# Last stage of a three-part kernel: PSUM split as four single banks and two pairs instead of two and three, and the last tile's output in two halves

## The chip, the cores and the metric

The kernel runs on one core of one Trainium2 chip. The metric is device time in microseconds (us) of one execution, the median of several runs. TensorE (PE) multiplies matrices into PSUM, which has eight banks of 512 fp32 values per partition here; VectorE (DVE) and ScalarE (ACT) read PSUM and work on tiles in SBUF; SyncE's queue (SP) issues the DMAs.

## The reference

Three parts follow each other: a block-causal attention (4 batches, 8 heads, 576 positions), a mixture of four experts over its 2304 output rows, and a feed-forward block with a SoLU and a layer norm, which is the last stage here:

```python
def _moe2_ref(x, w_in, w_out, g_ln) -> np.ndarray:
    h = x @ w_in                                  # 2304x512 @ 512x1024
    h_max = np.max(h, axis=-1, keepdims=True)
    e = np.exp(h - h_max)
    sm = e / (np.sum(e, axis=-1, keepdims=True) + 1e-09)
    solu = h * sm
    mu = np.mean(solu, axis=-1, keepdims=True)
    var = np.mean((solu - mu) ** 2, axis=-1, keepdims=True)
    ln = (solu - mu) / np.sqrt(var + 1e-06) * g_ln
    return (ln @ w_out).astype(np.float32)        # 2304x1024 @ 1024x512
```

## The kernel before

The 2304 rows are 18 tiles of 128. All products are made of fp16 pairs (a high and a low part), three matmuls for each product. The expert stage before the last one ends with second products of expert 3 (`emit_o`, L394, tiles named `ops`), which VectorE adds to the tile's sum (`out_unit`, L419, `acc`). ScalarE and VectorE then split that sum into an fp16 pair (L470, L471, `xh`), and a DMA transposes it to `x2T`, the input of the last stage. The PSUM tiles of the expert stage lie in a pool of three banks (`psh`, banks 0 to 2) and one of five (`psb`, banks 3 to 7); both are closed before the last stage opens its own two pools over the same banks, in the order in which they are written: `pso` first, then `ps2`.

The last stage runs over the 18 tiles t. `m2_h(t)` makes h: 24 matmuls of 512 columns (L1432) into a pair of banks of `ps2`. VectorE takes the maximum (L1438, `mx`) and a bias (L1442, `nb`); ScalarE the exponential with its sum (L1445, `ex`); VectorE the product h times ex (L1447, `raw`), which is the last reader of the pair. Then VectorE does the statistics (L1450, L1452), a chain of small instructions for the inverse root (L1455 to L1477), the normalisation (L1478), and with ScalarE the fp16 split (L1483 high part, L1484 low part, `lh`). SyncE issues the transposing DMA to `lt`. The tiles `ex`, `raw` and `lh` have two buffers each (pool `mp`), so `raw` of tile t+2 goes where `raw` of tile t lay until L1484 has read it. `m2_o(t)` makes the output: 24 matmuls (L1495) into a bank of `pso`, ScalarE copies it out with a scale (L1498, `o2s`), and SyncE issues the DMA to `out`. `m2_o` runs four tiles behind `m2_h` in the program (`OLAG = 4`).

A scheduler puts the instructions of each engine into a fixed order when the kernel is built; on the chip each engine takes its own instructions in that order and waits where an operand or a buffer isn't ready. I call the h of tile t h0, h1, ..., the output o0, o1, ..., and in the same way mx0, ex0, raw0, lh0, lt0. Before, `pso` holds banks 0 and 1, and the three pairs of `ps2` are banks 2-3, 4-5 and 6-7.

Of the kernel before, what the change touches and what calls it, by code (L numbers as in the profile page):

```python
# [7 lines left out]
F32 = mybir.dt.float32  # L8
# [6 lines left out]
AF = mybir.ActivationFunctionType  # L15
ALU = mybir.AluOpType
AX = mybir.AxisListType
PSUM = bass.MemoryType.PSUM

NB, NH, S, HD = 4, 8, 576, 64  # L20
NT, D, F, E = 2304, 512, 1024, 4
KD, KF = D // 128, F // 128
NTILE = NT // 128
# [14 lines left out]
TILES = [(0, 0), (2, 0)] + [(b, i) for b in range(NB) for i in range(1, 5)]  # L38
# [22 lines left out]
def tile_kernel(  # L61
# [16 lines left out]
    pe = nc.tensor  # L78
# [21 lines left out]
    vec, act, gp, sync = nc.vector, nc.scalar, nc.gpsimd, InOrder(nc.sync)  # L100
# [1129 lines left out]
    def norm():  # L1230
# [11 lines left out]
        w=p0[:5], x=p1[:5], W=p0[5:] + q0, X=p1[5:] + q1, P=[norm],  # L1242
        S=[lambda: at1.v_square(z0, 0, keep=True), lambda: at1.v_scale(z0, 1), lambda: at1.v_split(z0, 0)],
# [101 lines left out]
    while at1.more:  # L1345
        t, u, cost = moe[-1] if moe else (-1, None, 0)
        ok = t is None or t in ready and len(bg) <= n1
        if not ok or tdv <= tpe + 2.0:
            flush()
            at1.step()  # L1350
            a, c = at1.cost()
# [63 lines left out]
    mp = ctx.enter_context(tc.tile_pool(name="m2", bufs=2))  # L1415
    tp_ = ctx.enter_context(tc.tile_pool(name="lt", bufs=4))
    phs.close()
    pso = ctx.enter_context(tc.tile_pool(name="pso", bufs=2, space=PSUM))
    ps2 = ctx.enter_context(tc.tile_pool(name="ps2", bufs=3, space=PSUM))
    osc = sq.tile([128, 1], F32, tag="osc", name="osc")  # L1420
    vec.tensor_scalar_mul(osc, iw[:, 2 * len(LOADS) + 1:2 * len(LOADS) + 2], 1.0 / LSC)
    lnT = {}
# [64 lines left out]
        lnT[t] = tt  # L1487

    def m2_o(t):
        ps = pso.tile([128, 512], F32, tag="o2", name="o2")  # L1490
        tt, w = lnT.pop(t), wt["w_out"]
        m = 0
        for f in range(KF):
            for a, b in ((0, 0), (0, 1), (1, 0)):
                pe.matmul(ps, tt[:, a * KF + f], w[:, b, f], start=(m == 0), stop=(m == 3 * KF - 1))  # L1495
                m += 1
        o = ep.tile([128, 512], F32, tag="ev", name="o2s")
        act.activation(out=o, in_=ps, func=AF.Copy, scale=osc)  # L1498
        b, i = TILES[t]
        if i == 0:  # L1500
            for j in range(2):
                sync.dma_start(out=out[(b + j) * S:(b + j) * S + 64], in_=o[64 * j:64 * j + 64])
        else:
            r0 = b * S + 64 + 128 * (i - 1)
            sync.dma_start(out=out[r0:r0 + 128], in_=o)

    for t in range(NTILE + OLAG):
        if t < NTILE:
            m2_h(t)
        if t >= OLAG:  # L1510
            m2_o(t - OLAG)
# [69 lines left out]
```

## Time and profile before

| what | us |
|---|---|
| median of 3 runs (1112.07 to 1114.56) | 1113.18 |
| the profiled execution | 1114.37 |
| its span, first to last instruction | 1112.6 |
| PE busy | 1048.0 (94%) |
| DVE busy | 797.7 (72%) |
| ACT busy | 514.1 (46%) |
| POOL busy | 182.1 (16%) |

The profiled execution lasts 1.8 us longer than its span, and 1.2 us longer than the median of the runs. Times of instructions below are counted from the start of the span. "Busy" of PE is modelled from overlapping matmuls: one of 512 columns is shown with 379 ns, while 24 of them in a row take 5.18 us, 216 ns each. The granted clock is the share of TensorE's full speed (2.4 GHz) that it was given.

### The profile page before, as it was taken

What the parts mean: (1) busy time and instruction counts of PE and PEld (TensorE: products, weight loads), DVE (VectorE), ACT (ScalarE), POOL (GpSimd) and SP (SyncE); (2) the same over time, 40 slices, a digit from 0 to 9 for tenths busy, and PEclk for the clock granted to TensorE, in tenths of its full rate; (3) what the DMA queues carried; (4) which work ended last, traced back from release to release, by engine and by line L of the source; (5) the groups of instructions that cost most, each with busy time, mean ns of one, the idle gap of its engine ahead of it and who ended that gap; (6) DMA issues with size and microseconds to landing.
All of it is one profiled execution on the core that took longest, in us unless ns stands there. A gap on an engine that the chain in (4) does not pass through costs nothing.

```text
span 1112.6 us, 20532 instructions
## 1 busy us (share of the span) xinstructions
PE 1048.0 (94%) x8064; PEld 657.2 (59%) x8064; DVE 797.7 (72%) x1758; ACT 514.1 (46%) x1107; POOL 182.1 (16%) x176
## 2 busy tenths in 40 slices
PE   4579889799999999999999999999999999999998
PEld 4456666465555556555576767666667674444443
DVE  7898788738768677436677656674879558999883
ACT  5667676646755455433443424232446453333222
POOL 4874633422115421000000000000000000000000
PEclk9999989799999999999999999999999999999999
DMA  9868987928877857332531212330344311434333
GB/s 303 247 164 159 249 184 163 222 79 192 193 120 178 177 147 157 64 61 48 174 114 58 77 39 76 115 133 29 95 138 128 107 27 29 95 86 88 74 85 85
DMA packets 225600, 137.95 MB, mean 124 GB/s; under 512 B 184544, under 2 KB 192736, under 8 KB 225504
## 3 DMA queue, kind: packets, MB, share of 16 engines
q1 hardware_dynamic: 225504, 136.65, 50.2%
q8 instruction: 63, 1.03, 0.4%
q14 instruction: 33, 0.27, 0.1%
HBM read 79.47 MB, written 12.06 MB: 82 GB/s over the span
## 4 chain that ended last, share of the span: by engine, by line
PE 75%; DMA 9%; DVE 7%; POOL 4%; issue 2%; ACT 2%; SPq 0%; ACTq 0%; DVEq 0%; POOLq 0%
PE ops L394 29%; PE hps L626 13%; PE hps L372 11%; PE h L1432 8%; PE o L1495 8%; DMA pT<-hl 6%; PE pv L993 3%; PE sps L912 2%; DVE hl L964 1%; PE sps L915 1%; DVE wt L235 1%; POOL wt L228 1%; DMA spill<-acc 1%; POOL ks L792 1%; POOL qlo L792 1%
## 5 line engine op out<-in xcount | busy, mean ns | idle before, releaser
L394 PE MATMUL ops<-wt,hch 128*128 128x512 f16 x1728 | 396.1, 381 | 3.7 <-DVE wt L235 1.6
L394 PEld LDWEIGHTS <-hch 128*128 128x128 f16 x1728 | 166.8, 98 | 189.9 <-issue 11.0
L372 PE MATMUL hps<-xT,wt 128*128 128x384 f16 (+1 forms) x1536 | 216.3, 291 | 2.1 <-DVE hch L383 1.3
L372 PEld LDWEIGHTS <-wt 128*128 128x128 f16 x1536 | 126.9, 100 | 62.1 <-issue 6.7
L959 ACT ACTIVATE p<-sps,nm 128x320 f32<-128x320 f32 (+4 forms) x144 | 79.0, 553 | 78.3 <-DVE nm L928 58.7
L964 DVE TENSOR_TENSOR hl<-p,hl 128x320 f16<-128x320 f32 (+4 forms) x132 | 92.3, 718 | 30.4 <-ACT hl L963 29.8
L626 PEld LDWEIGHTS <-S 128*128 128x128 f16 x1152 | 96.0, 98 | 2.8 <-issue 0.5
L1432 PE MATMUL h<-wt,x2T 128*128 128x512 f16 x432 | 95.5, 379 | 1.8 <-DVE acc L419 1.8
L1495 PE MATMUL o<-wt,lt 128*128 128x512 f16 x432 | 95.5, 379 | 0.0
L235 DVE SCALAR_TENSOR_TENSOR wt<-stage,ws,wt 128x1024 f16<-128x1024 f32 (+1 forms) x64 | 85.3, 1346 | 6.1 <-ACT wt L232 4.4
L419 DVE SCALAR_TENSOR_TENSOR acc<-ops,coef,acc 128x512 f32<-128x512 f32 x54 | 40.4, 747 | 67.2 <-PE ops L394 67.1
L912 PE MATMUL sps<-ks,qhi 128*128 128x288 f32 (+3 forms) x160 | 70.6, 443 | 18.1 <-ACT p L959 7.8
L639 ACT ACTIVATE stu<-hps 128x384 f32<-128x384 f32 x72 | 34.5, 484 | 94.7 <-PE hps L626 94.6
L626 PEld LDWEIGHTS <-wt 128*128 128x128 f16 x864 | 72.9, 98 | 6.5 <-issue 0.6
L626 PE MATMUL hps<-T,S 128*128 128x192 f16 x864 | 76.5, 246 | 0.0
L383 DVE SCALAR_TENSOR_TENSOR hch<-hps,hch 128x384 f16<-128x384 f32 (+1 forms) x98 | 53.0, 541 | 29.8 <-ACT hch L382 29.6
L1432 PEld LDWEIGHTS <-x2T 128*128 128x128 f16 x432 | 42.3, 98 | 52.9 <-issue 2.1
L993 PE MATMUL pv<-v,pT 128*128 128x64 f16 x1392 | 54.8, 196 | 19.1 <-DMA pT<-hl 19.0
L1495 PEld LDWEIGHTS <-lt 128*128 128x128 f16 x432 | 42.3, 98 | 51.0
L382 ACT ACTIVATE hch<-hps 128x384 f16<-128x384 f32 (+1 forms) x98 | 47.1, 480 | 47.7 <-PE hps L372 47.4
L232 ACT ACTIVATE wt<-stage,ws 128x1024 f16<-128x1024 f32 (+1 forms) x56 | 59.8, 1094 | 18.8 <-DVE ws L140 15.2
L993 PEld LDWEIGHTS <-pT 128*128 128x128 f16 x1392 | 50.1, 100 | 30.1 <-DMA pT<-hl 23.0
(158 smaller groups left out, 1480.6 us busy)
## 6 DMA issues: line engine op xcount, KB each, us to landing
stage<-in_w_dram SPq DMA_DIRECT2D x50, 512.0 KB, 6.0
raw<-in_qT_dram SPq DMA_DIRECT2D x34, 256.0 KB, 3.4
vraw<-in_vC_dram SPq DMA_DIRECT2D x30, 256.0 KB, 3.3
raw<-in_kT_dram SPq DMA_DIRECT2D x24, 288.0 KB, 3.6
raw<-in_w_dram SPq DMA_DIRECT2D x24, 256.0 KB, 4.0
raw<-in_w_in_dram SPq DMA_DIRECT2D x8, 512.0 KB, 4.7
raw<-in_w_out_dram SPq DMA_DIRECT2D x8, 512.0 KB, 4.3
stage<-wf SPq DMA_DIRECT2D x8, 512.0 KB, 6.1
```

What stands on the lines that cost most here:

```text
L232: h = paced_a(bg_(act.activation(out=hi, in_=r, func=AF.Copy, scale=stage[key, "s"]), "A"))
L235: stage["last"] = vec.scalar_tensor_tensor(out=lo, in0=r, scalar=stage[key, "s"], in1=hi, op0=ALU.mult, op1=ALU.subtract)
L372: pe.matmul(ps[:, j * n:j * n + n], w[:, a, kk, f * 128:(f + 1) * 128], x[:, b * KD + kk, c0:c0 + n], start=(m == 0), stop=(m == 3 * KD - 1),)
L383: marks["D"] = nc.vector.scalar_tensor_tensor(out=h[:, 1, :n], in0=ps[:, :n], scalar=0.0, in1=h[:, 0, :n], op0=ALU.max, op1=ALU.subtract)
L394: pe.matmul(ps, hch[f][:, a, o0:o0 + 128], w[:, b, f, :], start=(m == 0), stop=(m == 3 * KF - 1))
L626: i = pe.matmul(ps[x][:, jj * HT:jj * HT + HT], lhs(a, kk, jj), rhs(b, kk), start=start, stop=(m == 5), skip_group_check=not first or jj > 0,)
L912: pe.matmul(o, q, rhs, start=True, stop=False)
L959: act.activation(out=dst, in_=src, func=AF.Exp, bias=nm[:, j + x:j + x + 1], scale=SCALE, accum_out=sums[:, h:h + 1],)
L964: anc["D"] = vec.tensor_tensor(out=hl[:, W + c0:W + c0 + n_], in0=pf[:, 0:n_], in1=hl[:, c0:c0 + n_], op=ALU.subtract)
L993: pe.matmul(o, tt[:, a * nch + c, :], v[:, bb, hs], start=(m == 0), stop=(m == total - 1))
L1432: pe.matmul(ps[:, half], x[:, a * KD + kk, c:c + 128], w[:, b, kk, half * 512:half * 512 + 512], start=(m == 0), stop=(m == 3 * KD - 1),)
L1495: pe.matmul(ps, tt[:, a * KF + f], w[:, b, f], start=(m == 0), stop=(m == 3 * KF - 1))
```

## The change

The pool of output banks goes from two tiles of one bank to four, and the pool of first products from three pairs to two. So `pso` now holds banks 0 to 3, and the two pairs of `ps2` are banks 4-5 and 6-7. For the last tile alone (t = 17) the output is made in two halves of 256 columns: 24 matmuls of 256 columns into one bank, a copy of 256 columns and a DMA of 128 KB, and then the same again for the other half with a second bank.

```diff
@@ -1415,8 +1415,8 @@
     phs.close()
-    pso = ctx.enter_context(tc.tile_pool(name="pso", bufs=2, space=PSUM))
-    ps2 = ctx.enter_context(tc.tile_pool(name="ps2", bufs=3, space=PSUM))
+    pso = ctx.enter_context(tc.tile_pool(name="pso", bufs=4, space=PSUM))
+    ps2 = ctx.enter_context(tc.tile_pool(name="ps2", bufs=2, space=PSUM))
@@ -1487,22 +1487,23 @@
     def m2_o(t):
-        ps = pso.tile([128, 512], F32, tag="o2", name="o2")
         tt, w = lnT.pop(t), wt["w_out"]
-        m = 0
-        for f in range(KF):
-            for a, b in ((0, 0), (0, 1), (1, 0)):
-                pe.matmul(ps, tt[:, a * KF + f], w[:, b, f], start=(m == 0), stop=(m == 3 * KF - 1))
-                m += 1
+        b, i = TILES[t]
         o = ep.tile([128, 512], F32, tag="ev", name="o2s")
-        act.activation(out=o, in_=ps, func=AF.Copy, scale=osc)
-        b, i = TILES[t]
-        if i == 0:
-            for j in range(2):
-                sync.dma_start(out=out[(b + j) * S:(b + j) * S + 64], in_=o[64 * j:64 * j + 64])
-        else:
-            r0 = b * S + 64 + 128 * (i - 1)
-            sync.dma_start(out=out[r0:r0 + 128], in_=o)
+        for c in [slice(0, 512)] if t < NTILE - 1 else [slice(0, 256), slice(256, 512)]:
+            ps = pso.tile([128, 512], F32, tag="o2", name="o2")[:, c]
+            m = 0
+            for f in range(KF):
+                for x, y in ((0, 0), (0, 1), (1, 0)):
+                    pe.matmul(ps, tt[:, x * KF + f], w[:, y, f, c], start=(m == 0), stop=(m == 3 * KF - 1))
+                    m += 1
+            act.activation(out=o[:, c], in_=ps, func=AF.Copy, scale=osc)
+            if i == 0:
+                for j in range(2):
+                    sync.dma_start(out=out[(b + j) * S:(b + j) * S + 64, c], in_=o[64 * j:64 * j + 64, c])
+            else:
+                r0 = b * S + 64 + 128 * (i - 1)
+                sync.dma_start(out=out[r0:r0 + 128, c], in_=o[:, c])
```

The scheduler moves instructions at two places on TensorE. The first is the passage from the expert stage into the last one. `ops_11565` is the last product of the expert stage, `h2_11636` is h0. Before:

```order
L216 MATMUL tp_11558<-wt1_11556,ones_87 128x1 [waits DVE_49]
...
L394 MATMUL ops_11565<-wt_10231,hch_11285 128x512 [waits DVE_49]
...
L394 MATMUL ops_11565<-wt_10231,hch_11319 128x512
L1432 LDWEIGHTS x2T_11601 [waits DMAHW6_49]
L1432 MATMUL h2_11636<-wt_10739,x2T_11601 128x512 [waits DVE_49]
```

And with the change:

```order
L216 MATMUL tp_11558<-wt1_11556,ones_87 128x1 [waits DVE_49]
L1432 LDWEIGHTS x2T_11601 [waits DMAHW6_49]
L1432 MATMUL h2_11636<-wt_10739,x2T_11601 128x512 [waits PE_49]
...
L394 MATMUL ops_11565<-wt_10231,hch_11285 128x512 [waits DVE_49]
...
L1432 MATMUL h2_11636<-wt_10739,x2T_11601 128x512
```

The first 12 matmuls of h0 now stand ahead of the 24 of `ops_11565`, the other 12 behind them, and the first no longer waits for VectorE.

The second place is TensorE at the fifth and sixth tile (`h2_11908` is h4, `h2_12005` is h5, and the `o2` tile made of `lt_11702` is o0). Before, 22 of the 24 matmuls of h5 stand between h4 and o0:

```order
L1432 LDWEIGHTS x2T_11603 [waits DVE_49]
L1432 MATMUL h2_11908<-wt_10739,x2T_11603 128x512 [waits PE_49]
...
L1432 LDWEIGHTS x2T_11603 [waits DVE_49]
L1432 MATMUL h2_12005<-wt_10739,x2T_11603 128x512 [waits PE_49]
...
L1495 LDWEIGHTS lt_11702 [waits DMAHW6_49]
L1495 MATMUL o2_11976<-wt_11605,lt_11702 128x512 [waits Activation_49]
```

With the change all of h5 stands behind o0, and h and o alternate from there on:

```order
L1432 LDWEIGHTS x2T_11603 [waits DVE_49]
L1432 MATMUL h2_11908<-wt_10739,x2T_11603 128x512 [waits PE_49]
...
L1498 LDWEIGHTS lt_11702 [waits DMAHW6_49]
L1498 MATMUL o2_11977<-wt_11605,lt_11702 128x512 [waits Activation_49]
...
L1432 LDWEIGHTS x2T_11603 [waits DVE_49]
L1432 MATMUL h2_12005<-wt_10739,x2T_11603 128x512 [waits PE_49]
```

The third place is VectorE, where nothing moves: the rows from the normalisation of tile 0 (`raw_11670`) to raw2 (`raw_11806`, made of h2, `h2_11772`) are the same in both kernels. `mx_11865` is mx3 and `lh_11699` is lh0.

```order
L1478 TENSOR_SCALAR raw_11670<-raw_11670,mv_11675,y_11684 128x1024 [waits DVE_49]
...
L1438 TENSOR_REDUCE mx_11865<-h2_11840 128x1 [waits PE_49]
...
L1484 TENSOR_TENSOR lh_11699<-raw_11670,lh_11699 128x1024 [waits Activation_49]
L1442 TENSOR_SCALAR nb_11869<-mx_11865,cs_11867 128x1 [waits DVE_49]
L1473 TENSOR_SCALAR z_11755<-z_11755 128x1 [waits DVE_49]
L1447 TENSOR_TENSOR raw_11806<-h2_11772,ex_11803 128x1024 [waits DVE_49]
```

raw2 stands behind lh0 in both; with two pairs, h4 goes into the pair that raw2 reads. Two smaller moves on VectorE: the third split of `w_out` (L235) now stands ahead of the L419 of `ops_11565`, and mx0 ahead of the last step of that tile's scale.

## Rows read from the trace of the kernel before

**Rows 1.** The page: busy us, share of the span and instructions of each engine.
```profile
PE 1048.0 (94%) x8064; PEld 657.2 (59%) x8064; DVE 797.7 (72%) x1758; ACT 514.1 (46%) x1107; POOL 182.1 (16%) x176
```

**Rows 2.** Chain that ended last, 860 to 1113 us: start, us, what.
```profile
1082.79 25.91 PE o L1495 x120
...
1108.78 0.69 ACT o2s L1498
```

**Rows 3.** Timeline, 900 to 930 us: start, us, engine, line, instruction, idle before.
```profile
914.94 5.34 PE L394 MATMUL ops<-wt,hch 128*128 128x512 f16 x24
...
922.05 8.15 PE L1432 MATMUL h<-wt,x2T 128*128 128x512 f16 x37 [1.77 <-DVE acc L419]
...
924.87 0.72 ACT L470 ACTIVATE xh<-acc,xs 128x512 f16<-128x512 f32 x1 [2.06 <-DVE xs L140]
```

**Rows 4.** Timeline, 922 to 1000 us: VectorE's and SyncE's large steps of tiles 0 to 4.
```profile
927.43 1.23 DVE L1438 TENSOR_REDUCE mx<-h 128x1 f32<-128x1024 f32 x1 [1.05 <-PE h L1432]
...
930.33 1.22 DVE L1447 TENSOR_TENSOR raw<-h,ex 128x1024 f32<-128x1024 f32 x1 [1.42 <-ACT ex L1445]
...
935.79 1.22 DVE L1447 TENSOR_TENSOR raw<-h,ex 128x1024 f32<-128x1024 f32 x1 [0.36 <-ACT ex L1445]
...
944.41 1.22 DVE L1484 TENSOR_TENSOR lh<-raw,lh 128x1024 f16<-128x1024 f32 x1
...
945.71 9.45 SPq L91 DMA_TRANSPOSE lt<-lh  x2
945.73 1.22 DVE L1447 TENSOR_TENSOR raw<-h,ex 128x1024 f32<-128x1024 f32 x1
...
952.58 1.23 DVE L1484 TENSOR_TENSOR lh<-raw,lh 128x1024 f16<-128x1024 f32 x1
...
953.84 1.22 DVE L1447 TENSOR_TENSOR raw<-h,ex 128x1024 f32<-128x1024 f32 x1
```

**Rows 5.** Busy time of VectorE in a stretch: us, busy (instructions), clock, DMA, GB/s.
```profile
930.33:945.73 15.40, 14.85 (x51) 1.00 0.00 0
```

**Rows 6.** All engines, two tiles' worth of six: busy (instructions) PE, PEld, DVE, ACT, POOL, clock.
```profile
953.00:1015.00 62.00, 62.00 (x289) 28.10 (x288) 58.58 (x181) 18.82 (x25) 0.00 (x0) 1.00 0.47 94
```

**Rows 7.** The instructions of tile lt: time from a transposing DMA's issue to its landing.
```profile
DMA to landing us min/median/max: 4.3/4.3/5.2
```

**Rows 8.** TensorE alone by stretches around its gaps: us, busy (matmuls), clock, DMA, GB/s.
```profile
118.90:121.20 2.30, 0.06 (x3) 1.00 0.91 115
121.20:130.00 8.80, 8.80 (x102) 1.00 1.05 276
...
151.00:153.60 2.60, 0.00 (x0) 1.00 0.63 153
153.60:160.20 6.60, 5.75 (x51) 0.50 1.02 268
...
197.00:203.10 6.10, 1.83 (x10) 0.58 1.19 239
203.10:211.40 8.30, 8.25 (x47) 0.50 0.89 214
...
269.70:271.80 2.10, 0.03 (x1) 1.00 0.99 87
...
273.30:276.70 3.40, 3.40 (x15) 0.53 0.89 203
```

**Rows 9.** Short matmuls, each with a weight load; copies of 512 and 256 PSUM columns.
```profile
806.70 4.12 PE L626 MATMUL hps<-T,S 128*128 128x192 f16 x48
...
L1498 ACT ACTIVATE o2s<-o,osc 128x512 f32<-128x512 f32 x18 | 12.3, 684 | 37.3 <-PE o L1495 27.4 <-issue 9.8
...
L382 ACT ACTIVATE hch<-hps 128x256 f16<-128x256 f32 x6 | 2.3, 386 | 0.9 <-PE hps L372 0.7
```

**Rows 10.** DMAs from 1108 us on: GB/s in 40 slices of 0.115 us; the last output.
```profile
GB/s 0 0 0 0 0 0 0 0 0 0 0 0 0 0 0 0 0 0 0 0 303 356 374 410 374 356 107 0 0 0 0 0 0 0 0 0 0 0 0 0
...
out_dram<-o2s SPq DMA_DIRECT2D x1, 256.0 KB, 2.0
```

## The prediction

> **What bounds the kernel now.** I read the page first. TensorE is busy for 94% of the span, VectorE for 72% [rows 1], so TensorE's gaps are where a change can win or lose. Then I read the timeline of the passage into the last stage. The last 24 matmuls of the expert stage begin at 914.94; at 216 ns each they are through at 920.12. h0 begins at 922.05 [rows 3], so 1.93 us are lost there (the row shows 1.77, since a matmul's end is modelled as later). The row names L419: h0's first pair, banks 2-3, shares a bank with that last product, and L419 has to read it first. From 922.05 the chain of waits runs over TensorE alone until the last matmul ends at 1108.70, which is its 864 matmuls at 216 ns and nothing else; behind it come ScalarE's copy of 0.69 us [rows 2] and the last DMA, 2.0 us from issue to landing [rows 10]. So the last stage has two things to give, 1.93 us at its start and a part of the tail. VectorE is the second engine to watch: from raw0 to raw2 it is busy for 14.85 of 15.40 us [rows 5].
>
> **The start gives 1.93 us.** By the new order 12 matmuls of h0 go at 914.94, the 24 of the expert stage at 917.53, the other 12 of h0 at 922.71, and h0 is complete at 925.31 instead of 927.23. Its pair is now 4-5, for which the order shows no wait on VectorE. I cost the later L419 at nothing: its tile belongs to 15 to 17, whose input is wanted 100 us later. The `w_out` splits are also done long before o0.
>
> **Two pairs cost 4.8 us.** With three pairs h3, h4 and h5 reuse the pairs of h0, h1 and h2. With two, h2 waits for raw0, h3 for raw1 and h4 for raw2. I walk it with the rows of before.
> - TensorE, with no wait, starts h1 at 925.31, h2 at 930.49, h3 at 935.67 and h4 at 940.86.
> - VectorE: mx0 and raw0 start at 927.43 and 930.33 now [rows 4], 0.2 and 3.1 us after h0's end. With h0 at 925.31 mx0 can start at 925.5, but ScalarE must also copy the last tile's `xh` (0.72 us [rows 3]) ahead of ex0, and the scalar for that copy now stands behind mx0. That takes some 0.6 us of the 1.9, so I let VectorE's sequence move 1.3 us earlier: raw0 ends at 930.33 - 1.3 + 1.22 = 930.25, in time for h2; raw1 ends at 935.79 - 1.3 + 1.22 = 935.7, just in time for h3.
> - raw2 does not fit. It stands behind lh0 in VectorE's order, and must, since it goes into the buffer of raw0. It starts at 945.73 now [rows 4], so at 944.4 then, and ends at 945.65. TensorE waits for it from 940.86 on: 4.8 us. The bounds: VectorE moves by all 1.93 us (the wait is 4.2) or not at all (6.1). I take 4.8, the walk's own value.
>
> Today this wait is hidden: h4 goes into the pair of h1, and h5, which needs raw2, starts at 948. What is queued behind the waiting matmul is all of TensorE's work, o0 included. Afterwards nothing is late: h4 runs from 945.7 to 950.9; lt0 lands 4.3 us [rows 7] after 945.71 even unmoved [rows 4], at 950.0, before o0. h5, at 956.1, needs raw3, which ends at 953.84 + 1.22 = 955.1 unmoved [rows 4]; o1, at 961.2, needs lt1, at 952.58 + 1.23 + 4.3 = 958.1. From there h comes every 10.36 us, and VectorE works 58.58 in 62.00 us, six tiles' time [rows 6], so it keeps up. Four output banks gain nothing: no o waits for one now.
>
> **The clock.** A gap of 4.8 us is longer than today's 1.9. In earlier stages TensorE went back to work at full clock after a gap of 2.3 us (from 118.9), at half (1.2 of 2.4 GHz) after one of 2.6 us (from 151.0), and at half after one of 2.1 us too (from 269.7) [rows 8]. At half clock work takes twice its time, so a stretch loses half its busy length: 3.40 us at 0.53 cost 1.6, 5.75 cost 2.9, 8.25 cost 4.1 [rows 8]. Nothing lost is the lower end, 4.1 the upper. I take 1.7, near the stretch of 273.3, because that gap too lies between dense work on both sides; the long stretches follow broken work.
>
> The Trainium skill (TensorE: Matmul & The Clock Gate, "Loop structure matters more than you think") says that a long wait between matmuls drops the clock to half, and that the next matmul then runs cold. By that rule the clock falls here for certain; the rows show it for two of the three gaps above, which are all shorter. Without the fall the sum would be 1.7 us less, the first rival below.
>
> **The tail gives 0.6 us.** The copy of 256 instead of 512 columns behind the last matmul: 0.684 against 0.386 for a 256-column copy from PSUM [rows 9], 0.3 us. The last DMA moves 128 KB instead of 256: the bytes take some 0.8 of the 2.0 us now, seven slices of 0.115 [rows 10], so up to 0.4 less, or nothing if the shorter 1 KB rows go at half the rate. I take 0.3. The first half's copy and DMA lie beside the second half's 24 matmuls, 2.6 us. The 24 extra weight loads stay hidden: 48 matmuls of 192 columns, each with its own load, take 4.12 us, 86 ns each [rows 9], less than the 108 ns of 256 columns. An upper bound for them is 0.1 us.
>
> The Trainium skill (Perfetto Trace Analysis, "DMA Optimizations") warns of pieces under 2 KB for their cost per transfer; no row here shows an output of 1 KB rows, and by it the DMA's 0.3 us would fall away.
>
> **The sum**: -1.93 + 4.8 + 1.7 - 0.6 = +4.0 us. The profiled execution would go from 1114.37 to 1118.4; it stands 1.2 us above the median, so the median goes from 1113.18 to **1117.2**.
>
> **Rivals.**
> - *The clock holds.* Everything else as above: +2.3 us, 1115.5. For it: the gap from 118.9 left the clock alone. Against it: this gap is twice as long. Chance 0.22.
> - *The clock stays low for long*, as in the stretch of 203.1: 4.1 instead of 1.7, +6.4 us, 1119.6. Against it: that stretch came after 6.1 us with little work. Chance 0.12.
> - *No wait for the pair, so faster.* If raw2 were done when TensorE comes to h4, only the gains stay: -2.5 us, 1110.7. It decides at 940.86: VectorE would have to be 4.8 us earlier at raw2. Against it: h0 is only 1.9 us earlier, and between raw0 and raw2 VectorE idles for 0.55 us in all [rows 5]. Chance 0.05.
> - *A partial wait*, around 2.5 us with the clock kept, if ScalarE and VectorE overlap better than in the trace: about 0, 1113.2. Chance 0.05.
> - *The first pair isn't free after all*, so that the change doesn't do what it says: the 12 matmuls of h0, now ahead of the expert stage's last product, would hold that up. The 1.93 us would stay lost, +5.9 us, 1119.1. Against it: the order shows no such wait. Chance 0.03.
>
> The forecast itself (a wait of 4 to 6 us, the clock low for a short while) has 0.53.
>
> **How the numbers follow.** The low end is the smallest wait, no lost clock and the whole tail: -1.93 + 4.2 - 0.7 = +1.6, 1114.8. The high end is the walk with the longest low clock and the copy's gain alone: -1.93 + 4.8 + 4.1 - 0.3 = +6.7, 1119.9. Between them lie the forecast, the first two rivals and the last; outside lie 0.10 and the edges. A difference of 0.2%, 2.2 us, is about what a measurement of this kernel can tell from none. Slower by more: the forecast, the long low clock, the unfree pair and half of the first rival, which lies on that edge, with a little taken off for noise: 0.77. Within: the other half, the partial wait and that noise, 0.19. Faster: most of the third, 0.04.
>
> **What would show it.** TensorE without a gap from 905 to 930; a gap of 4 to 6 us ahead of h4 near 941, released by L1447; no other gap later; the clock at 0.5 for some 3 us from there; the last matmul near 1113 after the span's start; a last copy of about 0.39 us. I am wrong if there is no gap ahead of h4, or if gaps come back at every tile, which would mean that VectorE can't keep up with two pairs.

## The result and the profile after

The changed kernel takes 1120.95 us (median of 4 runs, 1119.74 to 1121.59) against 1113.71 us for the kernel before in the same comparison (4 runs, 1112.07 to 1114.56): a ratio of 1.0066, with a 95% interval of 1.0048 to 1.0083. It is slower, as forecast, but the 1120.95 us lie above the forecast of 1117.2 and above the range's end of 1119.9.

The busy times of the changed kernel's page (they answer to [rows 1]; the 24 more instructions of PE are the last tile's second half):

```profile
PE 1049.7 (94%) x8088; PEld 660.2 (59%) x8088; DVE 800.8 (72%) x1758; ACT 513.5 (46%) x1108; POOL 179.7 (16%) x176
```

Apart from that the work of the engines is the same, and no busy time differs by more than 3.1 us. TensorE's timeline over the passage into the last stage and its first tiles (start us, us, engine, line, instruction, count, idle before; it answers to [rows 3]):

```profile
916.54 0.28 PE L216 MATMUL tp<-wt,ones 128*128 128x1 f32 x2
916.68 2.75 PE L1432 MATMUL h<-wt,x2T 128*128 128x512 f16 x12
919.27 5.34 PE L394 MATMUL ops<-wt,hch 128*128 128x512 f16 x24
924.45 18.29 PE L1432 MATMUL h<-wt,x2T 128*128 128x512 f16 x84
947.01 7.04 PE L1432 MATMUL h<-wt,x2T 128*128 128x512 f16 x24 [4.26 <-DVE raw L1447]
953.88 5.34 PE L1498 MATMUL o<-wt,lt 128*128 128x512 f16 x24
```

The 1.77 us of idle time ahead of h0 are gone: 12 matmuls of h0 run before the expert stage's last product, and h0 to h3 follow without a break. In their place h4 waits for raw2, with 4.26 us of idle time ahead of it, and its 24 matmuls are shown with 7.04 us where the other tiles have 5.34. After that TensorE waits no more: the next view has it busy for all of the 62.00 us from 954 to 1016, and the chain of waits, further down, runs over it to its last matmul.

TensorE by stretches (length, busy and matmuls, granted clock, DMA share, GB/s; it answers to [rows 8]):

```profile
942.70:947.00 4.30, 0.04 (x1) 1.00 0.02 3
948.10:951.50 3.40, 3.40 (x9) 0.50 0.45 84
951.50:954.00 2.50, 2.50 (x13) 1.00 0.06 12
954.00:1016.00 62.00, 62.00 (x289) 1.00 0.47 89
```

The clock holds through the gap and for the first microsecond of h4, and is then at half (1.2 of 2.4 GHz) for 3.4 us. From h4's start to o0's start there are 953.88 - 947.01 = 6.87 us for work of 5.18: 1.69 us lost.

VectorE's timeline, the steps that decide h4 (they answer to [rows 4]):

```profile
930.51 1.23 DVE L1447 TENSOR_TENSOR raw<-h,ex 128x1024 f32<-128x1024 f32 x1 [0.43 <-ACT ex L1445]
...
935.97 1.22 DVE L1447 TENSOR_TENSOR raw<-h,ex 128x1024 f32<-128x1024 f32 x1 [0.36 <-ACT ex L1445]
...
944.42 1.22 DVE L1484 TENSOR_TENSOR lh<-raw,lh 128x1024 f16<-128x1024 f32 x1
...
945.73 1.22 DVE L1447 TENSOR_TENSOR raw<-h,ex 128x1024 f32<-128x1024 f32 x1
```

raw2 stands directly behind lh0 and ends at 946.95; h4 starts at 947.01. Nothing is idle in between: from 944.42 on VectorE goes from one step to the next. From raw0 to raw2 it is busy for 14.75 of 15.22 us (14.85 of 15.40 in [rows 5]).

The end of the chain of waits (it answers to [rows 2]), and the last output's DMA (slices of 0.1 us from 1114 on; it answers to [rows 10]):

```profile
1088.73 25.98 PE o L1498 x144
...
1114.72 0.47 ACT o2s L1500
```

```profile
GB/s 0 0 0 0 0 0 0 0 0 0 0 0 0 0 0 0 0 0 0 0 82 328 369 328 185 21 0 0 0 0 0 0 0 0 0 0 0 0 0 0
...
out_dram<-o2s SPq DMA_DIRECT2D x1, 128.0 KB, 1.7
```

The last copy takes 0.47 us instead of 0.69, the last DMA 1.7 instead of 2.0.

So each step is there that the prediction names. What does not fit is the total: 7.2 us between the two medians, where the steps make 4. To see where the rest lies I divide each execution at the `tp` matmuls (L216), the last thing that TensorE does before the two orders part. Up to there the two programs are the same. Behind it, "stage" runs from the second of the two (0.03 us behind the start that the rows show) to the start of the last matmul, and "tail" from there to the end of the span. The table holds all kernels of this study, each with its profiled execution and, beside it, the ratio of its runs to runs of the kernel before in the same comparison; "against before" is the difference of stage and tail, in us and as a share of 1113.2 us.

| kernel | `tp` at | stage | tail | against before | ratio of runs, 95% interval |
|---|---|---|---|---|---|
| before | 914.80 | 193.48 | 4.28 | | |
| changed | 916.54 | 197.84 | 3.54 | +3.6, 1.0033 | 1.0066, 1.0048 to 1.0083 (4 runs) |
| e1, changed, repeated | 915.83 | 198.67 | 3.54 | +4.5, 1.0040 | 1.0040, 1.0022 to 1.0059 (10 runs) |
| e2, banks only | 912.26 | 197.68 | 4.28 | +4.2, 1.0038 | 1.0040, 1.0026 to 1.0054 (12 runs) |
| e3, halves only | 913.62 | 193.65 | 3.56 | -0.6, 0.9995 | 0.9986, 0.9969 to 1.0003 (12 runs) |
| e4, rotated, halves | 916.94 | 191.72 | 3.55 | -2.5, 0.9978 | 0.9977, 0.9962 to 0.9993 (12 runs) |
| e5, before, repeated | 915.99 | 193.48 | 4.28 | 0.0, 1.0000 | 1.0012, 0.9996 to 1.0027 (12 runs) |
| e6, three raw buffers | 915.38 | 196.92 | 3.54 | +2.7, 1.0024 | 1.0019, 1.0002 to 1.0035 (12 runs) |
| e7, gap filled | 915.15 | 196.16 | 3.54 | +1.9, 1.0017 | 1.0025, 1.0012 to 1.0038 (11 runs) |
| e8, rotated, whole | 913.17 | 191.55 | 4.29 | -1.9, 0.9983 | 0.9987, 0.9973 to 1.0000 (12 runs) |

The two first profiled spans, 1112.6 and 1118.0 us, differ by 5.4 us: 3.6 of them lie in stage and tail, and 1.7 ahead of `tp`, where the programs are the same.

### The profile page after: what moved, and what is told of

Its sections match the earlier page's. It is cut to its first block, busy times and chain, and to the rows that moved or that the text cites. A ratio compares the mean times of both kernels' runs of the same rounds, so it can differ in the third digit from the quotient of the medians.

```text
span 1118.0 us, 20585 instructions
## 1 busy us (share of the span) xinstructions
PE 1049.7 (94%) x8088; PEld 660.2 (59%) x8088; DVE 800.8 (72%) x1758; ACT 513.5 (46%) x1108; POOL 179.7 (16%) x176
## 4 chain that ended last, share of the span: by engine, by line
PE 71%; DVE 10%; DMA 9%; POOL 4%; issue 3%; ACT 2%; SPq 1%; DVEq 0%; ACTq 0%; POOLq 0%
PE ops L394 27%; PE hps L626 13%; PE hps L372 10%; PE o L1498 8%; PE h L1432 7%; DMA pT<-hl 4%; PE pv L993 3%; DMA stage<-in_w_dram 2%; PE sps L912 2%; PE sps L915 1%; DVE wt L235 1%; DVE hl L964 1%; SPq L91 1%; POOL wt L228 1%; DMA spill<-acc 1%
## 5 line engine op out<-in xcount | busy, mean ns | idle before, releaser
L1498 PE MATMUL o<-wt,lt 128*128 128x512 f16 (+1 forms) x456 | 95.6, 368 | 0.0
L235 DVE SCALAR_TENSOR_TENSOR wt<-stage,ws,wt 128x1024 f16<-128x1024 f32 (+1 forms) x64 | 86.2, 1361 | 6.6 <-ACT wt L232 5.0
L419 DVE SCALAR_TENSOR_TENSOR acc<-ops,coef,acc 128x512 f32<-128x512 f32 x54 | 40.4, 747 | 63.0 <-PE ops L394 62.9
L639 ACT ACTIVATE stu<-hps 128x384 f32<-128x384 f32 x72 | 34.5, 483 | 95.5 <-PE hps L626 95.4
L1498 PEld LDWEIGHTS <-lt 128*128 128x128 f16 x456 | 44.6, 98 | 48.9
L963 ACT ACTIVATE hl<-p 128x320 f16<-128x320 f32 (+4 forms) x132 | 65.0, 523 | 7.5 <-DMA pT<-hl 6.9
L382 ACT ACTIVATE hch<-hps 128x384 f16<-128x384 f32 (+1 forms) x98 | 46.9, 481 | 46.9 <-PE hps L372 46.7
```

The source lines that it names most:

```text
L235: stage["last"] = vec.scalar_tensor_tensor(out=lo, in0=r, scalar=stage[key, "s"], in1=hi, op0=ALU.mult, op1=ALU.subtract)
L963: anc["A"] = act.activation(out=hl[:, c0:c0 + n_], in_=pf[:, 0:n_], func=AF.Copy)
L1498: pe.matmul(ps, tt[:, x * KF + f], w[:, y, f, c], start=(m == 0), stop=(m == 3 * KF - 1))
```

## The experiments

Two sets of four kernels, each set on one chip with its own runs of the kernel before: 33 runs from 1111.05 to 1118.12, median 1115.77, beside e1 to e4; 35 runs from 1110.43 to 1119.40, median 1115.51, beside e5 to e8.

### e1: the changed kernel again

No edit. It asks whether the 3 us beyond the forecast come back.

> The changed kernel itself, unaltered, timed again. In its first profiled execution the last stage (from the end of the expert stage's second last product to the last matmul) took 198.0 us instead of 193.8, and what lies behind the last matmul 3.3 instead of 3.9: +3.7 in all. The other 1.7 us of that execution lie ahead of the last stage, and the medians differ by 7.2. Theory A (the change costs what the last stage shows, and the rest is the spread of the earlier stages between executions): a median 3 to 5 us above the kernel before. Theory B (the change also lengthens the stages ahead of it, by code or addresses): 6 to 9 us again, and the last stage of a new profile starts 1.5 us or more later than 914.9.

Measured: 1120.1 us against 1115.77, ratio 1.0040 (1.0022 to 1.0059). TensorE's timeline from h0's second half on, and its stretches around the gap:

```profile
923.74 18.29 PE L1432 MATMUL h<-wt,x2T 128*128 128x512 f16 x84
946.30 7.86 PE L1432 MATMUL h<-wt,x2T 128*128 128x512 f16 x24 [4.27 <-DVE raw L1447]
954.00 5.34 PE L1498 MATMUL o<-wt,lt 128*128 128x512 f16 x24
```

```profile
941.90:944.60 2.70, 0.13 (x1) 1.00 0.00 0
944.60:951.40 6.80, 5.09 (x13) 0.50 0.42 78
```

The gap is the same to 0.01 us. The clock falls earlier here, at 944.6, while TensorE still waits, and stays at half for 6.8 us, 5.09 of them at work; h4 loses 954.00 - 946.30 - 5.18 = 2.52 us instead of 1.69. The interval's ends are 2.4 and 6.6 us. The 4.0 us of the sum lie near the middle of it, the 7.2 of the first comparison outside. Theory A, 3 to 5 us, holds with 4.3; `tp` lies 1.0 us later than in the trace of before, where theory B wants 1.5 or more.

### e2 and e3: each half of the change alone

e2 has the new numbers of banks and the last tile whole; e3 has the old numbers and the last tile in halves.

```diff
-    pso = ctx.enter_context(tc.tile_pool(name="pso", bufs=2, space=PSUM))
-    ps2 = ctx.enter_context(tc.tile_pool(name="ps2", bufs=3, space=PSUM))
+    pso = ctx.enter_context(tc.tile_pool(name="pso", bufs=4, space=PSUM))
+    ps2 = ctx.enter_context(tc.tile_pool(name="ps2", bufs=2, space=PSUM))
```

> Only the two numbers of buffers changed (four output banks, two pairs); the last tile's output stays whole. Theory A: the gap ahead of h4 (4.3 us) and the low clock behind it (1.8 us lost) as in the changed kernel, the first product's 1.9 us gained, the tail as before: +4.3 us. Theory B, if the banks lengthen the earlier stages: +7 to +8.

> Only the last tile's output in two halves; two output banks and three pairs as before. Theory A: no gap ahead of h4, the 1.9 us ahead of h0 stay, the time behind the last matmul falls from 3.9 to 3.3 us: -0.6 us. Theory B, if the 48 added instructions on TensorE lengthen the earlier stages: +2 to +3.

Measured: e2 1119.49 us, ratio 1.0040 (1.0026 to 1.0054); e3 1112.78 us, ratio 0.9986 (0.9969 to 1.0003). TensorE's timeline of e2, and then that of e3:

```profile
942.73 7.04 PE L1432 MATMUL h<-wt,x2T 128*128 128x512 f16 x24 [4.27 <-DVE raw L1447]
949.61 5.34 PE L1495 MATMUL o<-wt,lt 128*128 128x512 f16 x24
```

```profile
913.76 5.34 PE L394 MATMUL ops<-wt,hch 128*128 128x512 f16 x24
920.88 30.81 PE L1432 MATMUL h<-wt,x2T 128*128 128x512 f16 x142 [1.77 <-DVE acc L419]
```

And the clock of e2 behind the gap:

```profile
943.70:947.10 3.40, 3.40 (x10) 0.51 0.49 92
```

The whole loss belongs to the banks: e2 has the gap of 4.27 us and the slow h4 with no halves, and e3 has neither, but the old gap of 1.77 us ahead of h0. The halves change the tail alone, from 4.28 to 3.56 us, and lengthen the stage by 0.17; the runs of e3 alone do not tell its 0.6 us from nothing, since their interval reaches to 1.0003.

### e4: the gain at the start without the loss at h4

Two output banks and three pairs as before, but the pairs are taken in the order 4-5, 6-7, 2-3, from three pools of one pair each; the last tile in halves. Apart from the halves, the edit against the kernel before is:

```diff
-    ps2 = ctx.enter_context(tc.tile_pool(name="ps2", bufs=3, space=PSUM))
+    ps2 = [ctx.enter_context(tc.tile_pool(name=f"ps2{c}", bufs=1, space=PSUM)) for c in "cab"]
...
-        ps = ps2.tile([128, 2, 512], F32, tag="h2", name="h2")
+        ps = ps2[(t + 1) % 3].tile([128, 2, 512], F32, tag="h2", name="h2")
```

> Three pairs as before and the halves, but the pairs are taken in the order 4-5, 6-7, 2-3, so that h0 goes over banks long free and h4 still has the pair of h1. Theory A: the 12 matmuls of h0 ahead of the expert stage's last product as in the changed kernel, no gap ahead of h0 and none ahead of h4 or h5 (h5 wants raw2 at 946.0 in the times of before, raw2 ends at about 945.7), clock full, tail 3.3: -1.9 - 0.6 = -2.5 us. A rival, that the gap of h4 comes from VectorE's backlog whatever the pairs: a gap of 1 us or more ahead of h5, so -1.5 or worse.

Measured: 1113.01 us against 1115.77, ratio 0.9977 (0.9962 to 0.9993): faster than the kernel before and than the changed one. TensorE's timeline and its clock:

```profile
917.08 2.75 PE L1432 MATMUL h<-wt,x2T 128*128 128x512 f16 x12
919.66 5.34 PE L394 MATMUL ops<-wt,hch 128*128 128x512 f16 x24
924.84 28.65 PE L1432 MATMUL h<-wt,x2T 128*128 128x512 f16 x132
```

```profile
915.00:1100.00 185.00, 185.00 (x860) 1.00 0.38 77
```

h0 starts as early as in the changed kernel, and there is neither a gap nor a fall of the clock afterwards. The rival, a gap of 1 us or more ahead of h5, did not come. The gain at the start comes from which banks the first pair lies in; the loss at h4 from how many pairs there are. The change tied the two together, and they need not be.

### e5: the kernel before again

No edit; its ratio should be 1, and its start shows the spread.

> The kernel before, unchanged, once more. What it tells apart is where the first comparison's 7.2 us came from. Theory A (the change costs about 4 us, all of it inside the last stage, and the rest is spread between executions that arises ahead of it): the ratio's interval holds 1.000; in the profiled execution the last stage, from the tp matmul of L216 to the last matmul's start, lasts 193.5 us again (to 0.3) and the tail 4.28, but the tp matmul itself can lie anywhere from 911 to 918 although the program is the same. Theory B (the start of 916.5 in two of the three traces with two pairs belongs to the change): the tp matmul lies at 914.8 again, within 0.5 us.

Measured: ratio 1.0012 (0.9996 to 1.0027), 12 runs from 1110.32 to 1119.76. Stage and tail repeat to 0.01 us. The start does not:

```profile
915.99 0.28 PE L216 MATMUL tp<-wt,ones 128*128 128x1 f32 x2
916.13 5.34 PE L394 MATMUL ops<-wt,hch 128*128 128x512 f16 x24
923.24 30.81 PE L1432 MATMUL h<-wt,x2T 128*128 128x512 f16 x142 [1.77 <-DVE acc L419]
```

The same program comes to the expert stage's last product at 916.13, 1.2 us later than in [rows 3]: theory B, which wants 914.8 to within 0.5, falls. Over the ten traces the `tp` matmuls lie between 912.26 and 916.94; the five with two pairs have a mean of 915.03 and lie 4.3 us apart, the five with three pairs have 914.90 and lie 3.8 us apart. So these traces show no shift of the start with the change, but the standard error of the difference of the two means is about 1 us, and a shift of up to 2 us could hide in them. The runs of e2 narrow it: their interval, +2.9 to +6.0 us, lies around the +4.2 us of stage and tail. Most of the spread is already there 400 us earlier: TensorE's last `pv` matmul of the attention starts between 511.21 (e2) and 515.95 (e4), and from there to `tp` it takes 400.3 to 401.8 us.

### e6: a third buffer for raw

raw2 stands behind lh0 because there are two `raw` buffers. With three the scheduler puts raw2 ahead.

```diff
-        raw = mp.tile([128, 2, 512], F32, tag="raw", name="raw")
+        raw = mp.tile([128, 2, 512], F32, tag="raw", name="raw", bufs=3)
```

> The changed kernel with three buffers for raw instead of two, so that raw2 needn't follow lh0 and stands ahead of it on VectorE. Theory A (h4 waits for raw2, whose time was set by the two raw buffers together with VectorE's backlog): by a walk with the durations of the trace of before, the gap ahead of h4 shrinks from 4.26 to about 0.7 us, but VectorE's work is only put in another order, so a new gap of about 3.2 us opens ahead of h5, which waits for raw3; in all 0.8 us less than the changed kernel's stage of 197.84, and up to 1.7 more if the clock holds: 195.3 to 197.0. Theory C (the wait has another cause than the pair's last reader, for instance the transposed input of h4): the gap ahead of h4 stays at about 4.3 and the stage at 197.8.

Measured: 1117.06 us against 1115.51, ratio 1.0019 (1.0002 to 1.0035). TensorE's timeline and its clock, then VectorE's large steps and its busy time:

```profile
923.29 18.29 PE L1432 MATMUL h<-wt,x2T 128*128 128x512 f16 x84
941.89 5.35 PE L1432 MATMUL h<-wt,x2T 128*128 128x512 f16 x24 [0.31 <-DVE r L1455]
950.10 6.39 PE L1432 MATMUL h<-wt,x2T 128*128 128x512 f16 x21 [2.85 <-DVE z L1473]
956.33 5.34 PE L1498 MATMUL o<-wt,lt 128*128 128x512 f16 x24
```

```profile
950.30:953.70 3.40, 3.40 (x9) 0.50 0.33 61
```

```profile
940.61 1.23 DVE L1447 TENSOR_TENSOR raw<-h,ex 128x1024 f32<-128x1024 f32 x1
...
946.26 1.21 DVE L1484 TENSOR_TENSOR lh<-raw,lh 128x1024 f16<-128x1024 f32 x1
...
948.83 1.22 DVE L1447 TENSOR_TENSOR raw<-h,ex 128x1024 f32<-128x1024 f32 x1
```

```profile
935.00:955.00 20.00, 20.00 (x75) 0.91 0.14 27
```

The gap ahead of h4 falls from 4.26 to 0.31 us, and one of 2.85 us opens ahead of h5, which starts 0.05 us after raw3's end at 950.05 (the rows name small steps of L1455 and L1473 that end just before; the pair's reader is raw). 1.1 of the 4.3 us of idle time are saved; the stage is 0.9 us shorter, 196.92, within the 195.3 to 197.0 of theory A. The buffer only set which tile has to wait; VectorE, which is busy for all of the 20 us from 935 to 955 in this trace, set how long. The clock falls after the gap of 2.85 us as it did after that of 4.26, and takes 1.7 us again: h5's 21 matmuls need 956.33 - 950.10 = 6.23 us instead of 4.53.

### e7: the gap filled with work

20 matmuls of 512 columns into a free output bank between h3 and h4; nothing reads what they compute. The rest is the changed kernel.

```diff
+        if t == 4:
+            fill = pso.tile([128, 512], F32, tag="o2", name="fill")
+            for m in range(20):
+                ins = pe.matmul(fill, x[:, 0, c:c + 128], w[:, 0, 0, 0:512], start=(m == 0), stop=(m == 19))
+                if m == 0:
+                    after(ins, h_end[0])
+            h_end.append(ins)
```

> The changed kernel with 20 more matmuls of 512 columns between h3 and h4, into a free output bank, whose result nobody reads; 20 at 216 ns take 4.32 us, the length of the gap. Theory A (of the loss at h4 4.26 us are the wait and 1.70 the lower clock that the idle engine is given): no gap over 0.2 us is left ahead of h4, the clock stays at 1.00, h4 takes 5.34 instead of 7.04 us on the timeline, and the stage falls from 197.84 to 196.1 (to 0.3), although TensorE has more to do. Theory D (h4 is slow for a reason of its own, such as its operands or the bank it writes): h4 still takes 7.0 us, and the stage is 197.8 or more.

Measured: 1117.76 us against 1115.51, ratio 1.0025 (1.0012 to 1.0038). TensorE's timeline, and its stretches:

```profile
923.06 18.29 PE L1440 MATMUL h<-wt,x2T 128*128 128x512 f16 x84
941.19 4.48 PE L1432 MATMUL fill<-wt,x2T 128*128 128x512 f16 x20
945.62 5.35 PE L1440 MATMUL h<-wt,x2T 128*128 128x512 f16 x24
```

```profile
941.20:945.60 4.40, 4.40 (x21) 1.00 0.01 2
945.60:951.00 5.40, 5.40 (x26) 1.00 0.52 97
```

With more work TensorE is through earlier: h4 starts when raw2 allows it, as before, but takes 5.35 us at full clock. The stage falls by 197.84 - 196.16 = 1.68 us, all of it the clock's part. h4's operands, banks and position are those of the changed kernel, so theory D falls: what was slow about it came with the idle time ahead.

### e8: the order of the pairs alone

The edit of e4's order in the kernel before, with the last tile whole.

> The kernel before (two output banks, three pairs, last tile whole) with one difference: the three pairs are taken in the order 4-5, 6-7, 2-3. Theory A (the 1.9 us at the start come from the first pair alone, and are lost only where a pair is dropped for it): h0 begins ahead of the expert stage's last product with no gap, h4 has no gap, the clock stays at 1.00; the stage is 193.48 - 1.9 = 191.6 (to 0.3) and the tail 4.28 as before, so 1.9 us or 0.17% less than before. Theory E (the start's gain comes back as a wait later, as VectorE is behind): a gap of 1 to 2 us appears at one of h3 to h5, and the stage stays at 193.5.

Measured: 1114.29 us against 1115.51, ratio 0.9987 (0.9973 to 1.0000). Stage 191.55, 1.93 us less than before, and tail 4.29. No gap and no lower clock:

```profile
913.31 2.75 PE L1432 MATMUL h<-wt,x2T 128*128 128x512 f16 x12
915.89 5.34 PE L394 MATMUL ops<-wt,hch 128*128 128x512 f16 x24
921.07 28.65 PE L1432 MATMUL h<-wt,x2T 128*128 128x512 f16 x132
```

```profile
915.00:1100.00 185.00, 185.00 (x859) 1.00 0.38 79
```

The gain at the start does not come back as a wait: with three pairs h5 is the first that needs raw2, and TensorE comes to it 5.2 us later than to h4: in e8 raw2 starts at 942.36 and takes 1.22 us, and h5 starts at 944.4. The runs alone barely tell the 1.9 us from nothing, since their interval ends at 1.0000; stage and tail do.

## Why the prediction was right and wrong

**The start, -1.93 us: right.** h0 begins ahead of the expert stage's last product, with no gap. e8, which changes nothing else, gives 193.48 - 191.55 = 1.93 us.

**The wait ahead of h4, 4.8 us: right in place and cause, 0.4 too long.** h0 to h3 start at 924.45 and take 84 times 0.216 us, to 942.59; h4 starts at 947.01, 4.42 us later (the row's 4.26 has the modelled end in it). Counted from `tp`, which lies 1.74 us later than in the trace of before, VectorE's raw0 moved from 930.33 to 928.77, 1.56 us, and raw2 from 945.73 to 943.99, 1.74 us. The prediction let the sequence move by 1.3 of the 1.93 us. ScalarE's copy did cost what was left of it at raw0, but by raw2 VectorE had most of that back. With 1.74 instead of 1.3 its walk gives 4.4. e6 shows that the other half of the argument, VectorE's full load, holds as well.

**The clock, 1.7 us: right.** 1.69 us in the changed kernel, 1.70 in e2, 2.52 in e1: that the first trace came within 0.01 us is luck, as its repeat shows. e7 takes the gap away and the 1.7 us with it, so they are the clock's and not h4's. The first rival, that the clock holds, falls: in the four traces with a gap of 2.85 us or more in this stage (the changed kernel twice, e2, e6) the clock fell every time. The Trainium skill (TensorE: Matmul & The Clock Gate, "Loop structure matters more than you think") says that a matmul behind a long wait runs cold: h4 agrees, with 0.50 from 948.1 to 951.5, though its first matmuls still ran at 1.00. The prediction called the fall certain by that section, whose example is a wait nearly twice as long as this one and which names no shorter one; that a wait of 4.3 us is enough, the traces here show. The prediction also misread one of its rows: behind the gap of 2.1 us from 269.7 TensorE did not go back to work at half. It worked for over a microsecond first, as h4 did, and the fall came about 273:

```profile
271.80:273.30 1.50, 1.50 (x19) 0.94 1.05 377
```

**The tail, -0.6 us: right, in other parts.** It went from 4.28 to 3.54 us. The two values differ by 0.74 from the last matmul's start; about 0.1 of that is the last matmul itself, 256 columns long instead of 512, which the longer stage of e3 gives back. From the last matmul's end it is 0.63. The copy gave 0.22 instead of 0.3 (it took 0.47, not the 0.386 of the other 256-column copy, which reads no scale tile: the last section has the rows), the DMA and the steps around it the remaining 0.4 instead of 0.3 (the DMA's own rows go from 2.0 to 1.7). The 24 extra loads stayed hidden: 144 matmuls take 25.98 us, where 120 took 25.91. The Trainium skill (Perfetto Trace Analysis, "DMA Optimizations") warns of pieces under 2 KB, and the prediction added that by it the DMA's 0.3 us would fall away. The trace shows a lower rate, in the best slice 369 GB/s with pieces of 1 KB against 410 with 2 KB, but half the bytes still landed 0.3 us earlier, so the measurement decides for the split.

**The sum: right.** -1.93 + 4.42 + 1.69 - 0.63 = +3.55, and +0.07 for the last five tiles' matmuls: the +3.6 us of the two traces, against +4.0 in the prediction; e1 has +4.5. The runs of e1 say +0.40%, which on 1113.2 us is +4.5.

**The time and its range: wrong.** The step that failed is the one from the sum to the time: "so the median goes from 1113.18 to 1117.2". It took the median of three runs as known, and the range was built from the costs of the last stage alone. Nothing in it stood for how far an execution, or a median of a few, lies from the next; it put that term at nothing and gave no reason. In 68 later runs the kernel before ranged from 1110.43 to 1119.40, with medians of 1115.77 and 1115.51, 2.3 to 2.6 us above 1113.18. On 1115.6 the same sum of +4.0 gives 1119.6, which is 0.5 from the repeat's 1120.1. The other 1.4 us lie in the four runs of the changed kernel: their median is 0.85 above that of ten more, and their interval, 1.0048 at the low end, does not hold the 1.0033 to 1.0040 that the traces show. It is the only one of the nine comparisons of which that can be said. On 1115.6 the range would have run from 1117.2 to 1122.3 and held the measured 1120.95; on the 1113.71 of the first comparison's own four runs it would have ended at 1120.4 and still missed, so the base alone does not account for it. The allowance of 0.2% for telling a change from none was 2.2 us, close to the shift of the base, but it went into the chances and not into the range.

Where the spread arises is shown only in part: most of it ahead of TensorE's last `pv` matmul, in a part of the program that no kernel here changes. There TensorE runs at half clock in stretches that add up to between 17 and 27 us in the ten traces; the two earliest, e2 and e8, have the least, but traces with the same sum still lie up to 3 us apart. What makes one execution's stretches longer wasn't tried. That the surplus of the first comparison is spread between executions is therefore argued, from the repeats, which do not show it again; whether its four runs of the kernel before lay low, and those of the changed kernel high, by chance or for another reason, such as the chip they ran on, stays open.

## What to carry to other kernels

When a buffer is taken from one pool to free another, ask which of its uses gains from the *place* and which from the *number*: here the gain of 1.9 us needed only another first pair of banks, and the loss of 6.1 us came only from there being two, so an order of pairs keeps the first without the second. Price a new gap on TensorE with the half clock behind it (1.7 to 2.5 us here, for a gap of 4.3; behind the old gap of 1.77 us the clock stayed at 1.00 in all three traces that have it), and look for the engine whose load sets the wait before adding buffers: a third `raw` buffer moved most of it to the next tile. And before a range is put on a time, put the spread of the executions into it: a sum that is right to half a microsecond is worth no more than the median of three runs that it is added to.

## What was not expected of the hardware

The same gap does not cost the same. After 4.26, 4.27 and 4.27 us without work the clock was at half for 3.4, 3.4 and 6.8 us, and h4 lost 1.69, 1.70 and 2.52 us: in the third the fall came 1.7 us before the work did, in the other two about 1 us after. In e6 a shorter gap, 2.85 us, cost the same 1.7 us as one of 4.26.

A copy of 256 columns out of PSUM took 0.47 us for the last stage's outputs (L1500) and 0.386 us in the expert stage (L382, [rows 9]), on the same engine and with the same number of elements. The outputs are fp32 and those of L382 fp16, but that is not the reason: in the trace of before, 384 columns out of PSUM take 484 ns into fp32 (L639) and 486 ns into fp16 (L382). (L382 takes a Relu and L639 a plain copy, so the function costs nothing there either.) What is left is the scale, which the last stage's copy reads from a tile (`osc`) and L382 does not. Two other copies of 512 columns, from fp32 into fp16, differ in that alone by their rows: 627 ns without a scale tile (L963) and 716 ns with one (L470, `xs`).

```profile
L382 ACT ACTIVATE hch<-hps 128x384 f16<-128x384 f32 x92 | 44.8, 486 | 46.8 <-PE hps L372 46.7
L639 ACT ACTIVATE stu<-hps 128x384 f32<-128x384 f32 x72 | 34.5, 484 | 94.7 <-PE hps L626 94.6
L470 ACT ACTIVATE xh<-acc,xs 128x512 f16<-128x512 f32 x18 | 12.9, 716 | 6.8 <-DVE xs L140 6.0 <-DVE xi L133 0.7
L963 ACT ACTIVATE hl<-p 128x512 f16<-128x512 f32 x4 | 2.5, 627 | 0.1
```

These 89 ns are about the 88 ns by which 474 lies above 386. No run changed the scale alone.
